# Folding the second sequence's odd rows a third time in a Fourier mixing kernel

## The chip, the cores and the metric

The kernel runs on one core of a Trainium2 chip. The metric is the device time of one execution in microseconds, the median of the runs.

## The reference

Eight sequences of 3008 rows and 256 columns go through a two-dimensional Fourier transform, of which the real part is kept, and then through a feed-forward layer with a squared ReLU:

```python
X = np.fft.fft(x, axis=1)            # x: 8 x 3008 x 256
X = np.fft.fft(X, axis=2).real
h = X.reshape(8 * 3008, 256) @ w_in  # 256 x 2048
r = np.maximum(h, 0.0)
out = (r * r) @ w_out                # 2048 x 256
```

## The kernel before

The transform along the columns is folded into the first weight matrix once, at the start (`G1`, `G2`, `gE`). What is left for each sequence b is the transform along the rows, for 1505 frequencies (the others mirror them). It gives three tiles: `Pt` (cosine part), `Qt` (sine part) and `Et` (one single column). They are allocated by `start`.

**Folding.** A row and its three mirror images arrive side by side in a tile `xt`. For each tile t, `fold(b, t)` makes five VectorE pieces (`s` at L420, `d` at L424, `sc` at L436, `dc` at L440 and `w` at L450, two instructions), and for some tiles a sixth, a `stream_shuffle` (L459). The result `folded[b, t]` has an even and an odd half, kp = 0 and 1. There are seven tiles in four classes: tile 0 (95 rows) and tile 1 (94) for classes 0 and 1, tiles 2 and 3 (`TWO`, 96 and 92) for class 2, and tiles 4 to 6 (`ODD0` on: 128, 128 and 120) for class 3, the odd rows. For b > 1 the odd rows come instead as four tiles 4 to 7 of 96 rows, two of them loaded in pieces of 32 and turned by the shuffle. Chains of VectorE and ScalarE pieces then fold them once more: `once` (pieces `begin`, `even`, `sine`, `odd`) and `twice` (`begin`, `even`, `sine`, `turned`, `copies`, `odd_v`, `odd_w`). `begin`, `sine` and `copies` are ScalarE work. Class 2 is folded by `once` in every sequence but the first. The chains are called `two`, `first` and `second` in `ahead`.

**The products.** `dft_ops(b)` makes a group of pieces for each part (which = 0 for `Pt`, 1 for `Qt`) and each kp: `even_n` and `odd_n` are matmuls into PSUM (tag "d", two buffers), and the joins (`join_4`, `join_2`, `join_1`, and `join_once`, `join_half`, `join_turned`) are VectorE work that reads them. `odd_n` multiplies class 3: for b = 1 by `product` (L567), three matmuls of 376 or 377 columns; for b > 1 by `twice_more` (L669), four of 94 or 95 columns. For that the table's columns are put in another order by `part_table` (ScalarE), after the last use in the old order. `dft_ops(None)` is the same transform for the single column of all later sequences at once; it reads `we`, which `scale_columns` (ScalarE) and `fold_columns` (VectorE, L398 and L400) make from 28 small loads (L391).

**The steps.** The feed-forward layer runs in 384 steps: 8 sequences x 6 blocks of 251 frequencies x 8 pairs of weight columns. In step i, `front` issues two halves h = 0 and 1, each with two matmuls into `ph` (L768, L769; two buffers) and three VectorE instructions (L771, L773, L774: the main work). ScalarE then does ReLU and square on `g` (L783, L784), GpSimd makes `s` (L791 to L794), and two steps later `back` issues seven matmuls (L821). After the last pair of a block, `gather` sums the products and two `store`s (transposes L887 and L888 on VectorE, then DMAs on SyncE's queue) follow in the steps with i % 8 equal to 3 and 4. Every matmul is in float32 and shows as two rows in the trace.

**What sets the order.** While sequence b runs, the pieces for b + 1 wait in a list `side`, written out by `ahead(b + 1)`. `between(h)` is called behind each half of `front` and takes pieces from the head of the list. Each has a nominal VectorE time. Zero-time pieces (matmuls, ScalarE work, allocations) are taken whenever they stand at the head on entry. The others are taken behind the second half of steps with a share, as long as the room of the slot and the pace allow; those in `from_psum` also elsewhere:

```python
SHARE = (1.2, 0.0, 0.0, 0.7, 0.7, 1.0, 1.0, 1.0)      # by i % 8
spent -= pace * share(i)                               # pace: sum of times / sum of shares
```

In the first sequence this begins with step 10, shares with step 12. All engines work through their instructions in the order in which they were issued. A tile load is issued on SyncE's queue by the `d` piece of an earlier tile (`load_later`, three ahead in the list `LATER`).

Of the kernel before, what the change touches and what calls it, by code (L numbers as in the profile page):

```python
# [82 lines left out]
def kernel(  # L83
# [13 lines left out]
    B, NROW, _, D = x.shape  # L97
# [11 lines left out]
    NT = len(TILES)  # L109
# [28 lines left out]
    ODD0 = NT - 3  # L138
    TWO = ODD0 - 2
# [12 lines left out]
    assert H == P and TILES[ODD0][0] == 3 and TILES[ODD0][3] >= ROWS2  # L152

    def load_x(b, t):
        if b > 1 and t >= ODD0:
            xt[b, t] = xp.tile([P, 4, D], F32, name="xt", tag="x")
            for p, first, count in ODD[t - ODD0]:
                nc.sync.dma_start(out=xt[b, t][p:p + count], in_=x[b, S // 8 + 1 + first:S // 8 + 1 + first + count])
            return
        c, r0, step, rows = TILES[t]  # L160
        if b and t == TWO + 1:
            xt[b, t] = xp.tile([P, 4, D], F32, name="xt", tag="x")
            for p in range(0, ROWS2, R):
                at = TILES[TWO][1] + step * (2 * HALF2 - p - R)
                nc.sync.dma_start(out=xt[b, t][p:p + R], in_=x[b, at:at + step * (R - 1) + 1:step])
            return

        while rows % 15 and rows % 16 and r0 + step * rows < NROW:
            rows += 1

        pool, tag = (gp, "g") if b == 0 and t < NT - NX else (xp, "x")
        xt[b, t] = pool.tile([P, 4, D], F32, name="xt", tag=tag)
        nc.sync.dma_start(out=xt[b, t][0:rows], in_=x[b, r0:r0 + step * (rows - 1) + 1:step])

    LATER = [(b, t) for b in range(1, B) for t in (TWO, TWO + 1, 0, *range(ODD0, NT if b == 1 else NL), 1)]

    def load_later(i):
        if i < len(LATER):
# [150 lines left out]
            tt(out=t4, in0=t2, in1=b21, op=ALU.subtract)  # L329


    folded, from_psum = {}, set()
    PQE = {}
    PART = (slice(0, H + 1), slice(H + 1, D))
    REVERSE = list(range(R - 1, -1, -1))
# [68 lines left out]
    def fold(b, t):  # L404


        odd, two = b > 1 and t >= ODD0, b > 0 and t == TWO + 1
        r = slice(0, ROWS2 if odd or two else TILES[t][3])
        st = {}

        def new(pool, nm, shape):
            st[nm] = pool.tile(shape, F32, name=nm, tag=nm)
            return st[nm]

        def f_s():
            nonlocal folds
            st["fs"] = sums[folds % 2]
            folds += 1
            v = xt[b, t]
            tt(out=st["fs"][r, :, 0:D], in0=v[r, 0::2], in1=v[r, 1::2], op=ALU.add)  # L420

        def f_d():
            v = xt[b, t]
            tt(out=new(fp, "fd", [P, 2, D])[r], in0=v[r, 0::3], in1=v[r, 1:3], op=ALU.subtract)  # L424
            if b > 0:
                load_later(LATER.index((b, t)) + NX)

        def halves():

            if b == 0 or "sc" not in st:  # L430
                st["sc"] = fp.tile([P, 2, D], F32, name="sc", tag="sc")
            return st["sc"]

        def f_sc():
            s = st["fs"]
            tt(out=halves()[r, :, PART[0]], in0=s[r, :, 0:H + 1], in1=s[r, :, D:H - 1:-1], op=ALU.add)  # L436

        def f_dc():
            d = st["fd"]
            tt(out=halves()[r, :, PART[1]], in0=d[r, :, 1:H], in1=d[r, :, D - 1:H:-1], op=ALU.subtract)  # L440

        def w_of(t):
            if (b, t) not in folded:
                folded[b, t] = wp.tile([P, 2, D], F32, name="w", tag="w")
            return folded[b, t]

        def f_w(part=slice(0, D)):
            v, w = st["sc"], w_of(t)
            for kp in range(2):
                tt(out=w[r, kp, part], in0=v[r, 0, part], in1=v[r, 1, part], op=ALU.subtract if kp else ALU.add)  # L450

        def f_e():
            nc.scalar.mul(lone[r, 2 * t:2 * t + 2, P - 1:], w_of(t)[r, :, H:H + 1], -1.0 if TILES[t][0] else 1.0)

        if b == 0:
            return [f_s, f_d, f_sc, f_dc, lambda: (f_w(PART[0]), f_e()), lambda: f_w(PART[1])]
        ops = [(0.7, f_s), (0.7, f_d), (0.5, f_sc), (0.4, f_dc), (0.9, f_w)]
        if odd and (t - ODD0) in (1, 2) or two:
            ops.append((0.7, lambda: nc.vector.stream_shuffle(w_of(t)[r], w_of(t)[r], REVERSE)))  # L459
        return ops  # L460
# [79 lines left out]
    def dft_ops(b):  # L540
# [7 lines left out]
        def group(kp, which):  # L548
# [138 lines left out]
            def odd_n():  # L687
                ps = psd.tile([P, 512], F32, name="pd", tag="d")[0:n]
                st["odd"] = ps[:, 0:n0]
                if b is None or b == 1:  # L690
                    return product(ps[:, 0:n0], 3)
                st["odd"] = twice_more(ps)

            def join_odd(what, nk):

                a, ps = st[what]
                nq = a.shape[-1]
                st[what] = o = hp.tile([P, NC[1][3]], F32, name="do", tag="do", bufs=1)[0:n, 0:nk]
                tt(out=o[:, 0::2], in0=a[:, 0:nq - 1], in1=ps[:, 0:nq - 1], op=ALU.add)
                if which == 1:  # L700
                    tt(out=o[:, 1::2], in0=ps[:, 1:nq], in1=a[:, 1:nq], op=ALU.subtract)
                else:
                    tt(out=o[:, 1::2], in0=a[:, 1:nq], in1=ps[:, 1:nq], op=ALU.subtract)
# [19 lines left out]
                return [((which, kp, nm), f) for nm, f in named]  # L723
            ops = [(0.0, even_n), (0.5, join_4), (0.7, join_2), (0.0, odd_n), (1.1, join_1)]
            from_psum.update((join_4, join_2, join_turned))
            join_once, join_half = (lambda: join_odd("odd", n0)), (lambda: join_odd("half", n1))
            from_psum.update((join_once, join_half))
            if b and b > 1:
                ops.insert(4, (0.7, join_once) if kp else (0.5, join_turned))
            if b and kp:  # L730
                ops.insert(2, (0.5, join_half))
# [22 lines left out]
    def load_e(b):  # L754
        nc.sync.dma_start(out=PQE[b][2], in_=e_dram[b:b + 1].to_broadcast([P, NKT]))
# [138 lines left out]

    def ahead(b):
        (_, start), *groups = dft_ops(b)
        tables = [(0.0, lambda tab=tab: part_table(tab, TWO if b == 1 else ODD0)) for tab in (cosT, sinT)]
        if b == 1:
            early = [(0.0, start), (0.0, take_turn), (0.5, make_turn)]
            middle = [(0.0, scale_columns), (1.0, fold_columns)] + dft_ops(None) + tables  # L900
        else:
            early, middle = tables if b == 2 else [], []
            groups = [(0.0, start)] + groups
        def woven(ops, chain):

            chain = list(chain)
            out = []
            for i, x in enumerate(ops):
                out += [x] + ([chain.pop(0)] if chain and i else [])
            return out + chain  # L910

        av, aw, bv, bw = range(ODD0, NL)

        def later(make):

            made = []

            def run(i):
                if not made:
                    made.extend(make())  # L920
                made[i]()

            return lambda times: [(x, lambda i=i: run(i)) for i, x in enumerate(times)]

        w = lambda t: folded[b, t]
        two = later(lambda: once(w(TWO), w(TWO + 1), BY_TWO))((0.0, 0.8, 0.0, 1.0))
        first = later(lambda: once(w(av), w(aw), BY_AC))((0.0, 0.8, 0.0, 1.0))
        second = later(lambda: once(w(bv), w(bw), BY_BD) + twice(w(av), w(aw), w(bv), w(bw)))(
            (0.0, 0.8, 0.0, 1.0, 0.0, 1.1, 0.0, 1.2, 0.0, 0.8, 0.8))
        if b == 1:  # L930
            return (early + fold(b, TWO) + fold(b, TWO + 1) + woven(fold(b, 0), two) + fold(b, ODD0) + middle
                    + fold(b, ODD0 + 1) + fold(b, ODD0 + 2) + fold(b, 1) + groups + [(0.0, lambda: load_e(b))])
        return (early + fold(b, TWO) + fold(b, TWO + 1) + woven(fold(b, 0), two) + fold(b, av) + fold(b, aw)
                + woven(fold(b, bv), first) + fold(b, bw) + woven(fold(b, 1), second)
                + groups + [(0.0, lambda: load_e(b))])

# [100 lines left out]
    def share(i):  # L1037
        return 0.0 if i < NJ + LAG + 2 else SHARE[i % NJ]

    def between(h):  # L1040


        nonlocal spent
        if i < NJ + LAG:
            return
        while side and not side[0][0]:
            side.pop(0)[1]()
        if h:
            spent -= pace * share(i)
        room = 1.9  # L1050
        while side and 0 < side[0][0] <= room and spent + side[0][0] / 2 <= 0:
            if not (h and share(i)) and side[0][1] not in from_psum:
                break
            t, f = side.pop(0)
            f()
            spent, room = spent + t, room - t

# [119 lines left out]
```

## Time and profile before

| | us |
|---|---|
| median of 3 runs | 1933.26 (1932.94 to 1933.3) |
| profiled execution | 1930.57 |
| its span | 1928.7 |
| TensorE busy | 1916.3 |
| VectorE busy | 1422.5 |
| GpSimd busy | 1105.5 |
| ScalarE busy | 950.3 |

The granted TensorE clock was 0.999. In the profile PE is the matmul part of TensorE and PEld its weight loads, which overlap matmuls; DVE is VectorE, ACT ScalarE, POOL GpSimd and SP SyncE. In a timeline a line gives the start in us, the duration in us, the engine, the source line and operation, output <- inputs with their shapes, the number of merged instructions, and in brackets the idle time before it with the engine and line that ended it. A matmul's duration includes its drain, so that neighbours overlap: the pace is read from start to start.

### The profile page before, as it was taken

The numbers are of one execution on the slowest core, as the hardware profiler recorded it, in microseconds if no ns is written. First come the engines' busy times: TensorE is split into PE (matmuls) and PEld (weight loads), VectorE is DVE, ScalarE is ACT, GpSimd is POOL, SyncE is SP. The second block draws the span as 40 slices with busy tenths as digits, with TensorE's granted clock in tenths as the row PEclk, the third lists the DMA queues.
The fourth block names the chain that finished last, engine by engine and source line by source line (L and its number), as shares of the span: only waits on it lengthen the run. The fifth ranks groups of instructions, "written<-read, shape, count | busy, mean of one in ns | idle before, by whom it ended". The sixth has DMA issues, their size and how long they took to land.

```text
span 1928.7 us, 28036 instructions
## 1 busy us (share of the span) xinstructions
PE 1916.3 (99%) x9258; PEld 1700.7 (88%) x9258; DVE 1422.5 (74%) x3595; ACT 950.3 (49%) x1179; POOL 1105.5 (57%) x1701
## 2 busy tenths in 40 slices
PE   9999999999999999999999999999999999999998
PEld 7888888888988888888988889888898888988887
DVE  8987767877677876787768777787777877655554
ACT  2855434555444554545444554445544555444443
POOL 0056555665566555666566565566656666566565
PEclk9999999999999999999999999999999999999999
DMA  7341111111111201121011110111111101100101
GB/s 225 115 43 32 33 23 45 36 28 31 28 36 28 47 12 29 35 47 28 12 35 36 39 28 12 44 39 36 21 18 47 36 12 22 28 12 12 22 12 22
DMA packets 145695, 69.53 MB, mean 36 GB/s; under 512 B 129228, under 2 KB 136342, under 8 KB 145549
## 3 DMA queue, kind: packets, MB, share of 16 engines
q1 hardware_dynamic: 145097, 66.83, 16.0%
q8 instruction: 73, 1.20, 0.3%
q14 instruction: 73, 0.60, 0.1%
q0 software_dynamic: 176, 0.65, 0.1%
q10 hardware_dynamic: 276, 0.26, 0.0%
HBM read 43.00 MB, written 24.69 MB: 35 GB/s over the span
## 4 chain that ended last, share of the span: by engine, by line
PE 95%; DVE 4%; issue 0%; DMA 0%; ACT 0%; DVEq 0%
PE ph L768 17%; PE ph L769 17%; PE mC L821 17%; PE mA L821 17%; PE mB L821 16%; PE mD L821 8%; PE pd L567 1%; PE pd L669 1%; PE pd L643 1%; DVE m L283 0%; DVE fd L281 0%; DVE w L450 0%; DVE he L771 0%; PE mA L808 0%; DVE fd L271 0%
## 5 line engine op out<-in xcount | busy, mean ns | idle before, releaser
L783 ACT ACTIVATE g<-g 128x1004 f32<-128x1004 f32 (+1 forms) x384 | 399.3, 1040 | 765.8 <-DVE g L774 445.0
L771 DVE SCALAR_TENSOR_TENSOR he<-Et,gE,ph 128x251 f32<-128x251 f32 (+1 forms) x768 | 363.0, 473 | 378.5 <-PE ph L769 373.4
L791 POOL TENSOR_TENSOR s<-g 128x251 f32<-128x251 f32 (+1 forms) x376 | 236.2, 628 | 686.5 <-ACT g L784 644.4
L768 PE MATMUL ph<-Pt,G 128*128 128x251 f32 (+1 forms) x1536 | 452.9, 376 | 0.0
L769 PE MATMUL ph<-Qt,G 127*128 127x251 f32 (+1 forms) x1536 | 452.0, 375 | 0.0
L784 ACT ACTIVATE g<-g 128x1004 f32<-128x1004 f32 (+1 forms) x384 | 399.3, 1040 | 12.2
L821 PE MATMUL mC<-s,wsum 128*128 128x251 f32 (+1 forms) x1504 | 381.7, 375 | 0.0
L821 PE MATMUL mA<-g,wout 128*128 128x251 f32 (+1 forms) x1504 | 380.0, 374 | 0.0
L773 DVE TENSOR_TENSOR g<-he,ph 128x251 f32<-128x251 f32 (+1 forms) x768 | 320.6, 417 | 53.3 <-POOL s L791 1.4
L769 PEld LDWEIGHTS ph<-Qt,G 127*128 127x128 f32 x1536 | 291.5, 190 | 35.8
L768 PEld LDWEIGHTS ph<-Pt,G 128*128 128x128 f32 x1536 | 285.7, 189 | 35.0 <-issue 0.6
L821 PEld LDWEIGHTS mC<-s,wsum 128*128 128x128 f32 x1504 | 285.6, 190 | 34.7
L821 PEld LDWEIGHTS mA<-g,wout 128*128 128x128 f32 x1504 | 282.9, 189 | 36.9 <-issue 1.3
L774 DVE TENSOR_TENSOR g<-he,ph 128x251 f32<-128x251 f32 (+1 forms) x768 | 314.3, 409 | 0.0
L792 POOL TENSOR_TENSOR s<-s,g 128x251 f32<-128x251 f32 (+1 forms) x376 | 270.4, 719 | 29.5
L793 POOL TENSOR_TENSOR s<-g 128x251 f32<-128x251 f32 (+1 forms) x376 | 271.4, 722 | 0.0
L794 POOL TENSOR_TENSOR s<-g,s 128x251 f32<-128x251 f32 (+1 forms) x376 | 238.7, 635 | 0.0
L821 PE MATMUL mB<-g,wsum 128*128 128x251 f32 (+1 forms) x752 | 220.5, 374 | 0.0
L821 PE MATMUL mD<-s,wout 128*128 128x251 f32 (+1 forms) x752 | 220.3, 374 | 0.0
L821 PE MATMUL mB<-s,wout 128*128 128x251 f32 (+1 forms) x752 | 219.9, 374 | 0.0
L821 PEld LDWEIGHTS mB<-g,wsum 128*128 128x128 f32 x752 | 142.6, 190 | 17.4
L821 PEld LDWEIGHTS mD<-s,wout 128*128 128x128 f32 x752 | 141.9, 189 | 17.7
(152 smaller groups left out, 1350.8 us busy)
## 6 DMA issues: line engine op xcount, KB each, us to landing
out_dram<-os SPq DMA_DIRECT2D x376, 56.0 KB
xt<-in_x_dram SPq DMA_DIRECT2D x37, 384.0 KB
xt<-in_x_dram SPq DMA_DIRECT2D x57, 128.0 KB
Et<-e_dram SPq DMA_DIRECT2D x7, 752.5 KB
out_dram<-os SPq DMA_DIRECT2D x288, 6.8 KB
raw<-in_moe_w_in_dram SPq DMA_DIRECT2D x16, 256.0 KB
raw<-in_moe_w_out_dram SPq DMA_DIRECT2D x16, 256.0 KB
xt<-in_x_dram SPq DMA_DIRECT2D x4, 512.0 KB
```

The source lines that it names most:

```text
L768: nc.tensor.matmul(hP, G1[:, fs], pt[:, ks], start=True, stop=True)
L769: nc.tensor.matmul(hQ, G2[0:P - 1, fs], qt[0:P - 1, ks], start=True, stop=True)
L771: nc.vector.scalar_tensor_tensor(out=t, in0=et[:, ks], scalar=gE[:, fc:fc + 1], in1=hP, op0=ALU.mult, op1=ALU.add)
L773: tt(out=g[:, h, 0, 0:n], in0=t, in1=hQ, op=ALU.add)
L774: tt(out=g[:, h, 1, 0:n][:, ::-1], in0=t, in1=hQ, op=ALU.subtract)
L783: act(v, v, AF.Relu)
L784: act(v, v, AF.Square)
L791: gt(out=s1, in0=g21, in1=g22, op=ALU.add)
L792: gt(out=s2, in0=s1, in1=g11, op=ALU.subtract)
L793: gt(out=s3, in0=g11, in1=g21, op=ALU.subtract)
L794: gt(out=s4, in0=g12, in1=s2, op=ALU.subtract)
L821: nc.tensor.matmul(acc[nm][:, i, 0:n], w, v[:, 0:n], start=j == 0 and i == 0, stop=j == NJ - 1, skip_group_check=True)
```

## The change

For b = 1 the odd rows take the path of the later sequences: four tiles of 96 rows, `once` and `twice` on them, `twice_more` in place of `product`, and the joins that go with it. The list for b = 1 becomes that of the others, with the column transform (`middle`) behind the first odd tile; `middle` now puts all four tables in the new order. `between` changes for all sequences: in its second loop zero-time pieces may follow at once in the same slot, save `even_n` and `odd_n` (the set `alone`), which still wait for the next call. In the first sequence a slot has room 2.4 in place of 1.9.

```diff
     def load_x(b, t):
-        if b > 1 and t >= ODD0:
+        if b and t >= ODD0:
...
-    LATER = [(b, t) for b in range(1, B) for t in (TWO, TWO + 1, 0, *range(ODD0, NT if b == 1 else NL), 1)]
+    LATER = [(b, t) for b in range(1, B) for t in (TWO, TWO + 1, 0, *range(ODD0, NL), 1)]
...
-    folded, from_psum = {}, set()
+    folded, from_psum, alone = {}, set(), set()
...
-        odd, two = b > 1 and t >= ODD0, b > 0 and t == TWO + 1
+        odd, two = b > 0 and t >= ODD0, b > 0 and t == TWO + 1
...
-                if b is None or b == 1:
+                if b is None:
                     return product(ps[:, 0:n0], 3)
                 st["odd"] = twice_more(ps)
...
             from_psum.update((join_4, join_2, join_turned))
+            alone.update((even_n, odd_n))
...
-            if b and b > 1:
+            if b:
                 ops.insert(4, (0.7, join_once) if kp else (0.5, join_turned))
...
-        tables = [(0.0, lambda tab=tab: part_table(tab, TWO if b == 1 else ODD0)) for tab in (cosT, sinT)]
+        tables = [(0.0, lambda tab=tab, t=t: part_table(tab, t)) for t in (TWO, ODD0) for tab in (cosT, sinT)]
         if b == 1:
             early = [(0.0, start), (0.0, take_turn), (0.5, make_turn)]
             middle = [(0.0, scale_columns), (1.0, fold_columns)] + dft_ops(None) + tables
         else:
-            early, middle = tables if b == 2 else [], []
+            early, middle = [], []
...
-        if b == 1:
-            return (early + fold(b, TWO) + fold(b, TWO + 1) + woven(fold(b, 0), two) + fold(b, ODD0) + middle
-                    + fold(b, ODD0 + 1) + fold(b, ODD0 + 2) + fold(b, 1) + groups + [(0.0, lambda: load_e(b))])
-        return (early + fold(b, TWO) + fold(b, TWO + 1) + woven(fold(b, 0), two) + fold(b, av) + fold(b, aw)
+        return (early + fold(b, TWO) + fold(b, TWO + 1) + woven(fold(b, 0), two) + fold(b, av) + middle + fold(b, aw)
                 + woven(fold(b, bv), first) + fold(b, bw) + woven(fold(b, 1), second)
                 + groups + [(0.0, lambda: load_e(b))])
...
-        room = 1.9
-        while side and 0 < side[0][0] <= room and spent + side[0][0] / 2 <= 0:
-            if not (h and share(i)) and side[0][1] not in from_psum:
+        room = 1.9 if i >= per else 2.4
+        while side and side[0][0] <= room and spent + side[0][0] / 2 <= 0:
+            t, f = side[0]
+            if f in alone or t and not (h and share(i)) and f not in from_psum:
                 break
-            t, f = side.pop(0)
+            side.pop(0)
             f()
             spent, room = spent + t, room - t
```

## The prediction

> **What bounds the kernel now.** I read the page first (its busy shares, then the chain that ended last), then a table of windows, one for each sequence, then the timeline of TensorE step by step, then VectorE around the places that the change fills. The page says that TensorE is the path:
>
> ```profile
> PE 1916.3 (99%) x9258; PEld 1700.7 (88%) x9258; DVE 1422.5 (74%) x3595; ACT 950.3 (49%) x1179; POOL 1105.5 (57%) x1701
> PE 95%; DVE 4%; issue 0%; DMA 0%; ACT 0%; DVEq 0%
> ```
>
> The windows say where it has no gap at all. Columns: window, then busy us and instructions of PE, PEld, DVE, ACT, POOL, the granted clock, the DMA share, GB/s:
>
> ```profile
> 60.00:300.00 240.00, 239.44 (x1134) 206.16 (x1133) 185.39 (x456) 124.21 (x168) 113.02 (x171) 1.00 0.24 49
> 300.00:540.00 240.00, 240.00 (x1163) 214.45 (x1162) 181.11 (x458) 121.28 (x151) 144.63 (x223) 1.00 0.14 31
> ```
>
> The reader is to see that the first sequence, from 60 us on, is as full as the second. So time is won only by taking TensorE work away, and lost only where TensorE is made to wait; VectorE has 55 us to spare in that window, on average.
>
> A busy TensorE hides its real pace, so I took the start of each step's first L768 matmul from the timeline. From step 12 (115.88 us) to the end, a step without transform matmuls takes 4.67 us, in every sequence. What a step takes above that is the price of the transform products in it. In the first sequence (which transforms the second one), steps 38 to 41, 44 and 46 take 0.89, 1.91, 2.80, 2.80, 0.88 and 1.89 us more: 11.17 us. In the second sequence, where the third one's odd rows are folded a third time, the sum is 1.79 + 0.90 + 0.90 + 0.89 + 0.89 + 0.88 + 0.88 = 7.13 us, and the four sequences after it have the same within 0.01. The difference lies in the odd products:
>
> ```profile
> 250.76 2.07 PE L567 MATMUL pd<-cosT,w 128*128 128x377 f32 x6
> 252.67 0.59 PE L768 MATMUL ph<-Pt,G 128*128 128x251 f32 x2
> ```
> ```profile
> 477.73 0.80 PE L669 MATMUL pd<-cosT,w 94*128 94x95 f32 x6
> 478.37 0.39 PE L669 MATMUL pd<-sinT,w 94*128 94x94 f32 x2
> 478.60 0.62 PE L821 MATMUL mA<-g,wout 128*128 128x251 f32 x2
> ```
>
> From start to start: three products of 377 columns (two rows each in the trace) take 1.91 us, four of 95 columns 0.87.
>
> **Part 1, TensorE.** `odd_n` for b = 1 goes from L567 to L669 in four groups (which 0 and 1, kp 0 and 1): 4 x (1.91 - 0.87) = 4.16 us. The step sums, which include the joints to the matmuls around, give 11.17 - 7.13 = 4.04 us; I take 4.04.
>
> A short product costs 0.109 us a row for 95 columns, against 0.318 for 377: so a thin product no longer pays by its columns.
>
> The Trainium skill ("TensorE: Matmul & The Clock Gate", "LDWEIGHTS (loading the stationary operand)") lets a weight load cost by its columns, 128/1.2 = 107 ns, however few rows, which speaks against thin folds; estimated by it the gain would be 4 x (1.91 - 8 x 0.107) = 4.2 us. By its streaming rule alone ("Back-to-back issue gap", N/2.4 + 2.5 ns), with two passes a row, it would be 4 x (1.91 - 0.67) = 5.0 us. The rows decide: 4.04.
>
> **Part 2, the pieces on VectorE.** Three folds of up to 128 rows become four of 96, with two shuffles, two `once`, one `twice` and four joins. I worked the rule of `between` through with both lists: the nominal sum for b = 1 rises from 41.2 to 55.7 us, the pace from 1.71 to 2.31 per unit of share, and with room 2.4 nearly every filled slot takes 1.6 to 2.3 nominal. In real time a slot can hold 2.3 us: 4.67 less two halves of main work at 1.17. What exceeds it makes VectorE late. TensorE bears some lateness: the second half's main work ends 3.46 us into its step (152.08 against 148.62), and its `ph` buffer is needed again at 4.67 + 0.85, so 2.1 us; `g` is done by ScalarE at 3.46 + 2.1 and is read by the back matmuls at 2 x 4.67 + 1.7, so over 5 us. So most slots cost nothing: the main work of the step covers them, and if that cover were gone the 15 us would be paid in part.
>
> One wait is tighter. The dealing rule moves the column transform (`scale_columns`, `fold_columns`, `dft_ops(None)`) from steps 25 to 30 to steps 21 to 24, and fills the slots ahead. Before, `fold_columns` stood alone in its slot:
>
> ```profile
> 189.84 0.26 DVE L398 TENSOR_TENSOR es<-xe 128x98 f32<-128x98 f32 x1
> 190.13 0.33 DVE L400 TENSOR_TENSOR we<-es 128x49 f32<-128x49 f32 x2
> 191.64 0.66 PE L567 MATMUL pd<-cosT,we 95*7 95x95 f32 x5
> ```
>
> `we` was ready 1.1 us before TensorE read it. After, I get: step 19 (`dc`, `w`, `two.odd`, then the store), step 20 (`s`, `d`, `sc`, store), step 21 (`dc`, `w`, `fold_columns`), and `even_n` behind the first front of step 22, where every `ph` matmul of the second front queues behind it on TensorE. Start from the same step 19 as now:
>
> ```profile
> 152.08 0.92 DVE L420 TENSOR_TENSOR fs<-xt 95x512 f32<-95x512 f32 x1
> 152.92 0.68 DVE L424 TENSOR_TENSOR fd<-xt 95x512 f32<-95x512 f32 x1
> 153.52 0.64 DVE L887 STREAM_TRANSPOSE os<-c 128x448 f32<-128x448 f32 x1
> 154.09 0.19 DVE L888 STREAM_TRANSPOSE os<-c 128x64 f32<-128x64 f32 x1
> 154.35 0.47 DVE L771 SCALAR_TENSOR_TENSOR he<-Et,gE,ph 128x251 f32<-128x251 f32 x1
> ```
>
> Mean paces from start to start over the trace: `s` 0.81, `d` 0.70, `sc` 0.45, `dc` 0.50, `w` 0.92, `once`'s odd 1.05, a store 0.78, the main work 2.34. Step 19: 152.08 + 0.50 + 0.92 + 1.05 + 0.78 = 155.33, one us later than the 154.35 above. Step 20: + 2.34 + 0.81 + 0.70 + 0.45 + 0.78 = 160.41. Step 21: + 2.34 + 0.50 + 0.92 + 0.29 + 0.2 = 164.66 for the half of `we` that is read first. TensorE comes to it at step 22 (162.65) + 0.85 = 163.50. It waits 1.2 us, and VectorE's main work for the second half comes that much later; by then VectorE has caught up, since step 22 lasts 7 us, and nothing is late next. With every op at its shortest pace there would be no wait, with every op at its longest 3.4 us; the ops are long and short by turns, so I take the means, 1.2, and 0.5 to 1.9 as likely.
>
> A second place: steps 35 to 39 hold `second`, where ScalarE's copies stand directly ahead of their VectorE readers. L509 and L510 take 0.46 us from start to last end, so VectorE waits some 0.6 in step 37 and 0.5 in step 38; its lateness grows 0.5, 1.2, 1.8, 2.2 over steps 35 to 38, and the last product of step 37's back, behind `sine`, relu and square on ScalarE and 2.65 us on GpSimd, comes within 0.2 of its due time. I take 0.2 lost, bounds 0 and 0.8. No gain is possible at either place: TensorE has no gap there now.
>
> **Part 3, what else moves.** All at nothing: the four tables (ScalarE, 1.7 us for two at 205.51, some 2.4 for the ODD0 pair that stood at 303.19) go to step 24, which lasts 8.1 us because two column products lie in it; uncovered they would hold back relu by 2 us, inside the 5. SyncE issues five more tile loads (eight for four tiles, in place of three), each after a `d`; its queue is behind until 138.90 us through the column loads (L391), and the first tile that comes this way is needed in step 20, at 157.7. The `e_dram` store and `load_e` go earlier. In later sequences, the zero-time pieces (`begin`, `sine`, `copies`) now run within a slot; worked through, no slot there exceeds 1.9 nominal, and VectorE is never more than 0.3 us late to a step there now.
>
> **Sum.** The profiled execution took 1930.57 us, of which 1928.7 span and 1.87 around it. -4.04 + 1.2 + 0.2 = -2.6: 1927.9 there. The median of the runs is 1933.26, 2.7 above the profiled one; the same difference gives 1930.6.
>
> **The rivals.** (a) Nobody waits: VectorE's ops come at their short paces, or the column transform lands a slot later than I dealt it. Then all 4.04 us show: 1929.2. For it: 55 us of free VectorE time. Against it: all the ops of three slots would have to be short at once.
> (b) Slower than before: ScalarE becomes the bound of the slots. Each zero-time piece that now runs within a slot (9 in the first sequence, 7 in each of six others) queues behind a relu and square pair of 2.1 us and VectorE waits for it with all behind it. It decides from where a slot plus its wait exceeds 2.3 + 2.1 us. If that cost TensorE 0.16 us for each of the 51, 8.0 us would go: 1933.3 - 4.0 + 8.0 = 1937.3. For it: the order on ScalarE is new everywhere. Against it: that pair ends about 1 us into the step, and the pieces run at 3.5.
> (c) The wait is larger: step 22 at 2.2, steps 37 to 39 at 0.8, and 1 us more in steps 28 to 32, which are as full: 1933.2, no difference.
>
> **How the numbers follow.** 0.2% is 3.87 us, about what a measurement of this kernel can tell from no change; (a) lies just beyond it, my sum within it. My sum with its bounds (1929.7 to 1931.9) has 0.55, (c) 0.15, (a) 0.20, (b) 0.10. Faster by over 0.2%: (a), 0.20. Within: 0.70. Slower: 0.10. The range reaches from (a) less 0.3 to (c) plus 1: 1928.9 to 1934.2.
>
> **What would show it.** Right: steps 38 to 47 carry 7.1 us above 4.67 each; a wait of PE for L400 near 163.6 of about 1.2 us; 24 fewer rows at L567 and 32 more at L669. Wrong: step 22 at 5.8 us (its product, no wait), or any gap of PE after 300 us.

## The result and the profile after

The changed kernel takes 1928.51 us (median of 13 runs, 1927.34 to 1929.80) against 1933.09 us for the kernel before (13 runs, 1931.24 to 1934.18): a ratio of 0.9977, 95% interval 0.9968 to 0.9985. It is faster by 4.6 us, 0.23% (by the interval, 2.9 to 6.2 us). The prediction was 1930.6 with a range from 1928.9 to 1934.2: the measured time lies 0.4 us below the range, and "faster by over 0.2%", which had 0.2, came true.

The profiled execution of the changed kernel took 1928.42 us, 1926.7 of them span. First the page: busy shares and instruction counts, then the shares of the chain that ended last.

```profile
PE 1912.0 (99%) x9266; PEld 1698.9 (88%) x9266; DVE 1444.1 (75%) x3633; ACT 956.0 (50%) x1201; POOL 1109.0 (58%) x1701
PE 95%; DVE 3%; DMA 1%; issue 0%; SPq 0%; ACT 0%; DVEq 0%
```

TensorE has eight rows more (32 at L669 in place of 24 at L567) and 4.3 us less busy time; VectorE has 22 us more and is still off the path. The windows (columns as before) miss 1.7 us of TensorE in the first sequence and nothing in the second. Cut finer, 1.5 us of that lie before 100 us (0.6 in the kernel before; step 10 begins 2.8 us later here), and 0.17 in step 22; from 170 us on there is no gap:

```profile
60.00:300.00 240.00, 238.30 (x1152) 206.94 (x1151) 202.40 (x502) 135.04 (x201) 115.56 (x172) 1.00 0.24 49
300.00:540.00 240.00, 240.00 (x1162) 214.47 (x1161) 182.47 (x458) 119.12 (x145) 144.94 (x224) 1.00 0.14 32
```

The timeline of TensorE, step 40 of the first sequence, has thin products where L567 stood with 377 columns:

```profile
258.49 0.62 PE L769 MATMUL ph<-Pt,G 128*128 128x250 f32 x2
258.95 0.59 PE L770 MATMUL ph<-Qt,G 127*128 127x250 f32 x2
259.37 0.80 PE L669 MATMUL pd<-cosT,w 94*128 94x95 f32 x6
260.01 0.39 PE L669 MATMUL pd<-sinT,w 94*128 94x94 f32 x2
260.24 1.04 PE L822 MATMUL mA<-g,wout 128*128 128x251 f32 x4
```

The four products take 0.87 us from start to start (259.37 to 260.24), as they did in the later sequences of the kernel before.

The two executions are compared by the starts of the steps, as in the prediction (line numbers behind the diff are one higher: `front` is L769 now). Excess over 4.674 us a step, in us:

| | before | after |
|---|---|---|
| transform products for the second sequence | 11.17 (steps 38 to 46) | 7.12 (steps 40, 41, 44 to 46) |
| column transform | 6.91 (steps 28, 29) | 7.16 (steps 22 to 24: 1.51, 2.20, 3.45) |
| steps 35 to 39 without products | 0 | 0 |
| start of step 10 to start of step 383 | 1803.91 | 1800.10 |
| start of step 383 to the end of the execution | 20.14 | 18.96 |

So -4.05 + 0.25 = -3.8 us in the steps, all of it before step 48 (from there to step 383 both take 1608.2 us), and -1.2 us behind them, of which the prediction knew nothing. (The last row counts the 1.8 us or so that the execution takes around its span; inside the span it is 18.26 and 17.20.) Together -5.0. The rest of the difference between two single executions is the start: step 10 began at 106.52 us in the kernel before and at 109.36 in the changed one. That start varies from execution to execution: over the traces below step 10 begins from 106.5 to 111.8 us with the old schedule (mean of six 109.0) and from 108.0 to 110.3 with the new one (mean of eight 108.8). No part of the gain is shown there.

Two questions were left. Why did TensorE wait 0.3 us for `we` and not 1.2? And are the 1.2 us at the end a part of the change?

### The profile page after: what moved, and what is told of

It reads as the page before. It is cut to its first block, busy times and chain, and to the rows that moved or that the text cites. A ratio compares the mean times of both kernels' runs of the same rounds, so it can differ in the third digit from the quotient of the medians.

```text
span 1926.7 us, 28110 instructions
## 1 busy us (share of the span) xinstructions
PE 1912.0 (99%) x9266; PEld 1698.9 (88%) x9266; DVE 1444.1 (75%) x3633; ACT 956.0 (50%) x1201; POOL 1109.0 (58%) x1701
## 4 chain that ended last, share of the span: by engine, by line
PE 95%; DVE 3%; DMA 1%; issue 0%; SPq 0%; ACT 0%; DVEq 0%
PE ph L769 17%; PE ph L770 17%; PE mC L822 16%; PE mA L822 16%; PE mB L822 16%; PE mD L822 8%; PE pd L567 1%; PE pd L669 1%; PE pd L643 1%; DMA cosT<-in_cos_s_dram 0%; DVE he L772 0%; DMA cosd<-in_cos_d_dram 0%; DVE m L283 0%; DVE fd L281 0%; DVE g L775 0%
## 5 line engine op out<-in xcount | busy, mean ns | idle before, releaser
L792 POOL TENSOR_TENSOR s<-g 128x251 f32<-128x251 f32 (+1 forms) x376 | 237.1, 631 | 692.4 <-ACT g L785 635.5
L769 PE MATMUL ph<-Pt,G 128*128 128x251 f32 (+1 forms) x1536 | 452.6, 375 | 0.0
L769 PEld LDWEIGHTS ph<-Pt,G 128*128 128x128 f32 x1536 | 285.3, 189 | 35.1 <-DVE g L775 1.1
L795 POOL TENSOR_TENSOR s<-g,s 128x251 f32<-128x251 f32 (+1 forms) x376 | 240.5, 640 | 0.0
```

The source lines that it names most:

```text
L769: nc.tensor.matmul(hP, G1[:, fs], pt[:, ks], start=True, stop=True)
L792: gt(out=s1, in0=g21, in1=g22, op=ALU.add)
L795: gt(out=s4, in0=g12, in1=s2, op=ALU.subtract)
```

## The experiments

**The new rule alone.** The kernel before, with only the diff's changes to `between`, to `alone` and to its two uses:

```diff
-        room = 1.9
+        room = 1.9 if i >= per else 2.4
...
+            if f in alone or t and not (h and share(i)) and f not in from_psum:
```

> The kernel before with the new rule of between alone (alone, room 2.4, zero-time pieces within a slot); the second sequence keeps its three odd tiles and the direct odd products. Theory 1 (TensorE's products are the whole gain): steps 38 to 46 still carry 11.17 us above 4.67 each, steps 22 to 29 6.9 us for the column transform, later sequences 7.13 each; time as before within 0.3 us. Theory 2 (the gain beyond 4.0 us comes from the rule, which lets ScalarE's pieces start earlier): 0.5 to 1 us faster than before. Rival (b) of the prediction (the rule makes VectorE wait for ScalarE in the slots): 1 us or more slower, and steps above 4.67 in the later sequences.

1932.12 us, ratio 0.9996 (0.9987 to 1.0005). Steps 10 to 383 take 1803.89 us, as before; the products take 11.17 in the same steps; the column transform moves to steps 25, 28 and 29 and takes 6.92. Rooms of 2.4 and zero-time pieces within a slot move work and cost nothing. The median is 0.9 us under that of the kernel before, as theory 2 had it, but not in the steps: the stretch behind the start of step 383 takes 18.91 us in place of 20.14, which the last experiments take up.

**The old rule in the later sequences.** The changed kernel, where zero-time pieces may follow within a slot in the first sequence only:

```diff
-            if f in alone or t and not (h and share(i)) and f not in from_psum:
+            if f in alone or i >= per and not t or t and not (h and share(i)) and f not in from_psum:
```

> The kernel after, but from the second sequence on zero-time pieces again wait for the next call, as before the change. Theory 1: nothing in the later sequences depends on it, 7.13 us above 4.67 in each and the same time as after, within 0.3 us. Theory 2: 0.5 to 1 us slower than after.

1927.34 us, ratio 0.9974 (0.9964 to 0.9985). Steps 10 to 383: 1800.11, as the changed kernel. With the run above this ends rival (b): the new order on ScalarE costs nothing that the steps show, in any sequence.

**The column transform one fold later.** It stands behind the second odd tile:

```diff
-                ... + woven(fold(b, 0), two) + fold(b, av) + middle + fold(b, aw)
+                ... + woven(fold(b, 0), two) + fold(b, av) + fold(b, aw) + middle
```

> The kernel after with the column transform one tile later in the list (behind tile 5 in place of tile 4): fold_columns is then dealt alone in step 24 and TensorE reads we in step 25, where VectorE is not late. Theory 1: the wait of 0.34 us for L400 is gone and the column transform costs 6.9 us in its steps in place of 7.16; the rest is the same; 0.3 us faster than after by the steps, too little for the runs to show. Rival (the 0.25 us more in steps 22 to 24 come from how the products are split over the steps, not from VectorE): still 7.1 to 7.2 us.

1927.57 us, ratio 0.9971 (0.9959 to 0.9982). `we` is ready at 177.9 us, nobody waits for L400, and the column transform takes 3.45 + 3.46 = 6.91 in steps 25 and 28. Steps 10 to 383: 1799.85, 0.25 less than the changed kernel. So the whole of the wait was worth 0.25 us. By its steps this version is the fastest of those that compute everything; the 0.25 is too small for the runs, where the one before has the lower median (1927.34).

**More VectorE work ahead of the two tight places.** `f_w` (two L450) is issued once more in the slot ahead of `we`, and twice more in step 38:

```diff
+        again = lambda ops: [(0.0, ops[4][1])] if b == 1 else []
+        f_av, f_1 = fold(b, av), fold(b, 1)
+        last = woven(f_1, second)
+        last = last[:-1] + again(f_1) * 2 + last[-1:]
-                ... + fold(b, av) + middle + fold(b, aw) + ...
+                ... + f_av + again(f_av) + middle + fold(b, aw) + ... + last
```

> The kernel after with the two instructions of L450 done once more in step 21, ahead of fold_columns, and twice more in step 38 (same values written again; nothing left out). If VectorE works at its short pace there (0.67 us for the pair), step 22 grows by 0.67 us, from 6.18 to 6.85; at the mean pace of the prediction (0.92) to 7.1; if TensorE did not wait for VectorE there it stays at 6.18. In step 38 the lateness at the start of step 39 grows from 1.55 us by 1.35 to 1.85; by the prediction's count of ph buffers what exceeds 2.4 us is lost, 0.5 to 1.0 us around steps 39 and 40; if the tolerance is larger, nothing.

1933.33 us (one run). Step 22 rises from 1.51 to 2.62; steps 39 and 40 carry 2.54 and 3.55 in place of 0 and 1.79, so 4.3 us. Both costs are above what was expected (0.67 to 0.9 and 0.5 to 1.0): both places were sensitive, but the size depends on what stands beside the added work. The timeline of VectorE at both places:

```profile
164.88 1.42 DVE L450 TENSOR_TENSOR w<-sc 96x256 f32<-96x256 f32 x4
...
166.51 0.78 DVE L400 TENSOR_TENSOR we<-es 128x49 f32<-128x49 f32 x2
...
255.23 3.33 DVE L450 TENSOR_TENSOR w<-sc 94x256 f32<-94x256 f32 x4
```

The same four instructions took 1.42 us in step 21 and 3.33 in step 38, and the pair L400 0.78 in place of the 0.33 it takes in the changed kernel. GpSimd and TensorE in the second place:

```profile
255.85 0.81 POOL L795 TENSOR_TENSOR s<-g,s 128x251 f32<-128x251 f32 x1
256.62 0.81 POOL L792 TENSOR_TENSOR s<-g 128x251 f32<-128x251 f32 x1
257.51 0.77 POOL L793 TENSOR_TENSOR s<-s,g 128x251 f32<-128x251 f32 x1
...
259.85 0.69 PE L769 MATMUL ph<-Pt,G 128*128 128x250 f32 x2 [2.37 <-DVE g L775]
```

GpSimd ran one instruction after the other beside the slow four; beside the quick four it was idle (an instruction ended at 164.57, the next began at 166.47). The last line measures the tolerance: VectorE came 4.80 us late to step 39 (its main work began 5.85 us behind the step's first matmul, in an undisturbed step 1.05) and TensorE waited 2.37, so the `ph` buffer of the first half forgives 2.4 us (the prediction worked out 2.1 for the second).

**GpSimd silent.** The changed kernel without GpSimd's L792 to L795 in the first sequence; `back` reads `g` there:

```diff
+        if i < per:
+            return g.rearrange("p a b n -> p (a b) n")
```

> The kernel after, but in steps 8 to 47 GpSimd's combination (L792 to L795) is left out and the back matmuls read g in place of s; the rest of the first sequence is issued as in after. Theory (VectorE instructions with two SBUF inputs take their short pace, 0.60, 0.33 and 0.34 us, when GpSimd is idle and up to twice that when they meet one of its instructions): dc at the head of steps 19 and 21 falls from 0.69 and 0.81 us to 0.33, we comes some 0.8 us earlier, the wait of 0.34 us in step 22 is gone (6.9 us above 4.67 in steps 22 to 24 in place of 7.16), VectorE starts step 39 less than 1.2 us late in place of 1.55. Rival (the first instruction behind L775 is slow because L774 and L775 read PSUM ahead of it): dc stays at 0.69 to 0.81, the wait stays within 0.1 us.

1928.29 us (one run). Steps 10 to 383: 1799.99. Slot 21 of VectorE, to be read beside that of the changed kernel further down:

```profile
163.45 0.41 DVE L440 TENSOR_TENSOR sc<-fd 96x254 f32<-96x254 f32 x1
163.89 0.76 DVE L450 TENSOR_TENSOR w<-sc 96x256 f32<-96x256 f32 x2
164.57 0.25 DVE L398 TENSOR_TENSOR es<-xe 128x98 f32<-128x98 f32 x1
164.86 0.33 DVE L400 TENSOR_TENSOR we<-es 128x49 f32<-128x49 f32 x2
```

`dc` at the head of the slot takes 0.41 us in place of 0.77; lateness at the starts of steps 20 and 21 falls from 0.57 and 0.41 to 0.26 and 0.10, and at step 39 from 1.55 to 0.26; the wait for L400 is gone and the column transform takes 6.93. The rival, which put the long `dc` down to VectorE's own reads of PSUM ahead of it, would have kept it. The pieces of slot 20 keep their paces (0.60, 0.60, 0.34 and 0.69 for the store, against 0.60, 0.61, 0.33 and 0.69): there GpSimd did not hinder them in the changed kernel either.

**Both together.** The added work of the run before the last, and GpSimd silent (the two diffs above in one).

> The kernel with the repeated work in steps 21 and 38, and again without GpSimd's combination in steps 8 to 47 (left out, g read in place of s). Theory: the four L450 in step 38, 3.3 us beside GpSimd, take 1.35 us; VectorE starts step 39 some 2.3 us late, within the 2.4 that the ph buffers allow, and the 4.3 us lost in steps 39 and 40 fall below 0.3; step 22 loses at most 0.2 us. Rival: the four keep 2.5 us or more and TensorE loses 1.5 us or more in step 39.

1928.60 us (one run). The four L450 of step 38 take 1.42 us (3.33 beside GpSimd), VectorE is 1.60 us late to step 39, and steps 39 and 40 carry no wait: 11.13 us together, against 15.43 with GpSimd at work and 11.14 in the changed kernel. Step 22 still loses 0.17. So 4.3 us of TensorE's time hung on whether GpSimd worked beside these four VectorE instructions and the pieces ahead of them (without the added work the lateness at step 39 is 1.55 us with GpSimd and 0.26 without).

**Both kernels again.** For the end of the run, the kernel before and the changed kernel without any edit:

> The kernel before, unchanged, measured like the others: a ratio of 1.000 with an interval that says what such a comparison can resolve, and a second profile of the start. Theory (the start varies from execution to execution, the steps do not): step 10 begins anywhere between 105 and 113 us, and from there to the start of the last step it takes 1803.9 us within 0.1, as in the first profile. Rival (the steps vary as well): more than 0.3 us of difference between the two profiles.

1933.64 us, ratio 1.0001 (0.9992 to 1.0010); steps 10 to 383 in 1803.92, end 20.20 us.

> The kernel after, unchanged. By the steps it is 3.81 us faster than before (1800.10 against 1803.91 us from step 10 to step 383), so 0.9980; the first comparison gave 4.6 us. If the 0.8 us more are the scatter of the start, the median falls between 1928 and 1930.5 and the ratio between 0.9970 and 0.9988, and the profile again shows 1800.1 us between these steps with step 10 anywhere between 105 and 113 us. If after starts earlier by itself, step 10 begins near 108.5 again and the ratio stays at or below 0.9977.

1927.81 us against 1933.18, ratio 0.9972 (0.9962 to 0.9982); steps in 1800.11, end 19.08 us. Steps and ends repeat; what varies is the start.

**ScalarE's instructions shifted.** The end differs in one place: the last store's two DMA issues on ScalarE's queue. In the kernel before, and in the changed one:

```profile
1923.59 2.44 ACTq L879 DMA_DIRECT2D out_dram<-os  x2
```
```profile
1922.62 1.09 ACTq L880 DMA_DIRECT2D out_dram<-os  x2
```

In the kernel before, a packet of the queue q14, of the kind `instruction`, falls into that stretch. DMA queues between 1923.5 and 1926.1 us (packets, MB, share of the 16 engines):

```profile
q1 hardware_dynamic: 283, 0.26, 33.4%
q10 hardware_dynamic: 66, 0.07, 7.9%
q14 instruction: 1, 0.01, 1.6%
```

Three kernels shift ScalarE's stream by instructions that write the same small values again at 109 us (nine or eighteen more of L344, 0.19 us each), and a control adds six on VectorE (L350):

```diff
-                nc.scalar.mul(turn[r, a, i:i + 1], ...)
+                for _ in range(2):                        # range(3) for eighteen
+                    nc.scalar.mul(turn[r, a, i:i + 1], ...)
```
```diff
-            tt(out=to, in0=u, in1=v, op=op)
+            for _ in range(3):
+                tt(out=to, in0=u, in1=v, op=op)
```

> The kernel before, with nine more ScalarE instructions that write the same values again (each instruction of take_turn, L344, is issued twice; 0.19 us each, near 109 us). It tells whether the last 1.2 us of the gain belong to the change. By the steps the changed kernel wins 3.8 us; the rest of what was measured lies behind the start of step 383, where the kernel before takes 20.14 and 20.20 us to the end and the changed one 18.9 to 19.1. There ScalarE's two last DMA issues take 2.44 and 2.54 us against 1.09, and a packet of the instruction queue falls between them. Theory F (instruction fetch): ScalarE's stream of instructions is fetched in pieces, and a piece ends between the two issues in the kernel before; nine more instructions ahead move that point. Steps 10 to 383 as before, 1803.9 us (bound 0.3), the two issues 1.1 us, the end 19.0 us: 1.1 us faster than before. Rival W (the work): the longer end goes with the schedule of the kernel before, whatever ScalarE's stream is: 2.4 to 2.5 us for the issues and 20.1 to 20.2 for the end, time as before. Both: no other step changes.

1931.31 us against 1933.16, ratio 0.9991 (0.9982 to 1.0001). By the runs alone this is no sure difference, and the steps are those before (1803.92), but the end falls from 20.14 to 18.77 us. ScalarE's queue, then the DMA queues from 1925.0 to 1927.5 us:

```profile
1925.07 1.09 ACTq L880 DMA_DIRECT2D out_dram<-os  x2
```
```profile
q1 hardware_dynamic: 283, 0.26, 34.9%
q10 hardware_dynamic: 276, 0.26, 33.5%
```

No packet of q14 there, and the issues take 1.09 us.

> As the run with nine more ScalarE instructions, with eighteen (each of L344 is issued three times). Theory F: the point between two pieces moves further; the two issues take 1.1 us and the end 19.0 us, unless the point falls on them again. Rival W: 2.4 to 2.5 us and 20.1 to 20.2 us. Steps 10 to 383: 1803.9 us by both, up to 0.5 more if 3.4 us of ScalarE work at step 10 holds a relu back.

1930.00 us (one run): steps 1803.91, issues 1.09, end 18.82 us.

> The changed kernel with eighteen more ScalarE instructions (each of L344 is issued three times). Theory F: a shift of ScalarE's stream alone can make the end longer or leave it; two sizes of shift in the kernel before and one here, so a long end (issues of 2 us or more, end of 19.8 to 20.2) here would show that the schedule has no part in it. Rival W: the end stays at 18.9 to 19.1 us. Steps 10 to 383: 1800.1 us by both.

1929.39 us (one run): steps 1800.09, issues 1.10, end 19.00 us. This shift met no packet, so by itself it tells neither theory from the other.

> Control: the kernel before, with six more instructions on VectorE in place of ScalarE (each of make_turn, L350, is issued three times, 0.15 us each, near 119 us). If the fetch in question is that of ScalarE's stream, the end stays at 20.1 to 20.2 us and the two issues at 2.4 to 2.5 us. If any change in the program moves it (fetches of all engines share the queue), it may go to 19.0. Steps 10 to 383: 1803.9 us.

1933.83 us (one run): steps 1803.91, end 20.32 us. ScalarE's queue, and q14 between 1926.6 and 1929.1 us:

```profile
1926.67 2.39 ACTq L880 DMA_DIRECT2D out_dram<-os  x2
```
```profile
q14 instruction: 1, 0.01, 1.7%
```

All fourteen traces, with the stretch from 0.3 us ahead of the two issues to 1.8 us behind their start:

| kernels | q14 packet there | two issues, us | end, us |
|---|---|---|---|
| before, before again, six more on VectorE | yes | 2.44, 2.54, 2.39 | 20.14, 20.20, 20.32 |
| before with the rule alone, with 9, with 18 | no | 1.08, 1.09, 1.09 | 18.91, 18.77, 18.82 |
| changed, again, old rule later, `we` later, more work, 18 | no | 1.08 to 1.10 | 18.96 to 19.08 |
| GpSimd silent, and with more work | yes | 1.96, 2.21 | 19.77, 20.04 |

The long end comes with both schedules and leaves the old one when nine ScalarE instructions are added. So the last 1.2 us are no work that the change saved: they come and go with the packet. In the five traces that have it there, the packet begins between 0.21 us ahead of the start of the first of the two issues and 0.38 behind it, so beside the first and not between the two; that first issue takes 1.30 to 1.88 us in place of 0.38, the second 0.62 in place of 0.67. The other queue of this kind, q8, has no packet that begins within 4 us of them in any of the fourteen. Whether the packet itself holds the issue up, and whether it carries ScalarE's instructions, no run tests apart. Which counts of which instructions put the packet there is open too: the rule alone removed it with the same 1179 busy instructions on ScalarE, and the kernels with GpSimd silent brought it back with the changed kernel's 1201.

## Why the prediction was wrong

**Part 1 was right.** -4.04 was worked out from two step sums, and -4.05 came.

**The wait for `we` was the mis-sized term**: 1.2 us, measured 0.34 (by the pace of the matmul ahead TensorE was due at 166.34 and started at 166.68), of which 0.25 shows in the steps. The place, the step and the instructions were as worked out. VectorE in the changed kernel:

```profile
154.92 0.65 DVE L440 TENSOR_TENSOR sc<-fd 95x254 f32<-95x254 f32 x1
155.61 0.76 DVE L450 TENSOR_TENSOR w<-sc 95x256 f32<-95x256 f32 x2
156.29 0.87 DVE L495 SCALAR_TENSOR_TENSOR w<-w,turn,f 94x256 f32<-94x256 f32 x2
...
160.05 0.68 DVE L420 TENSOR_TENSOR fs<-xt 96x512 f32<-96x512 f32 x1
160.65 0.68 DVE L424 TENSOR_TENSOR fd<-xt 96x512 f32<-96x512 f32 x1
161.26 0.42 DVE L436 TENSOR_TENSOR sc<-fs 96x258 f32<-96x258 f32 x1
...
164.64 0.77 DVE L440 TENSOR_TENSOR sc<-fd 96x254 f32<-96x254 f32 x1
165.45 0.76 DVE L450 TENSOR_TENSOR w<-sc 96x256 f32<-96x256 f32 x2
166.12 0.25 DVE L398 TENSOR_TENSOR es<-xe 128x98 f32<-128x98 f32 x1
166.41 0.33 DVE L400 TENSOR_TENSOR we<-es 128x49 f32<-128x49 f32 x2
```

and TensorE, which waits for the first half of `we` (the 0.17 in the line counts from the end of the drain of the matmul ahead):

```profile
166.68 1.14 PE L567 MATMUL pd<-cosT,we 95*7 95x95 f32 x8 [0.17 <-DVE we L400]
```

The changed kernel's step 19 starts 2.85 us later than that of the kernel before (151.47 against 148.62), so the prediction's walk starts at 152.08 + 2.85 = 154.93; `dc` began at 154.92. From there, in us (from each start to the next):

| stretch | predicted | measured |
|---|---|---|
| slot 19: `dc`, `w`, odd and store | 0.50 + 0.92 + 1.83 = 3.25 | 0.69 + 0.68 + 1.48 = 2.85 |
| step 20: main work, `s`, `d`, `sc`, store | 2.34 + 0.81 + 0.70 + 0.45 + 0.78 = 5.08 | 2.28 + 0.60 + 0.61 + 0.33 + 0.69 = 4.51 |
| step 21: main work, `dc`, `w`, `es`, half of `we` | 2.34 + 0.50 + 0.92 + 0.29 + 0.2 = 4.25 | 2.36 + 0.81 + 0.67 + 0.29 + 0.2 = 4.33 |
| sum | 12.58 | 11.69 |

0.89 us too much, and 1.2 - 0.89 is the 0.3 that came. The failed step is the choice of means for the pieces. For those with two inputs in SBUF a mean over the whole trace mixes two kinds of slots: short where GpSimd is idle (`s` 0.60, `sc` 0.33, `w` 0.67), long beside it. Those kinds don't come by turns at random, as I took them to. (Of the 0.89, 0.18 are the two stores, at 0.69 in place of 0.78. They take 0.69 with GpSimd silent too; why the mean is higher was not looked into.) Around slots 19 to 21, GpSimd's four instructions have ended before the slot begins or within 0.5 us of its start, and the next step's begin only when VectorE's main work and ScalarE are done:

```profile
159.35 0.63 POOL L795 TENSOR_TENSOR s<-g,s 128x251 f32<-128x251 f32 x1
162.44 0.63 POOL L792 TENSOR_TENSOR s<-g 128x251 f32<-128x251 f32 x1 [2.46 <-ACT g L785]
```

All of slot 20 (160.05 to 162.28) lies in the gap between these two, 159.98 to 162.44; in slots 19 and 21 only the `dc` at the head meets an L795 (in slot 19 the store's transposes meet an L792 as well and keep their 0.64 and 0.20 us). This is no rule for late slots: VectorE is 0.59 us late to step 37, and there GpSimd runs on for 1.8 us of the slot, so that L495 takes 1.33 us in place of 0.87:

```profile
246.75 1.33 DVE L495 SCALAR_TENSOR_TENSOR w<-w,turn,f 94x256 f32<-94x256 f32 x2
246.86 0.95 POOL L794 TENSOR_TENSOR s<-g 128x251 f32<-128x251 f32 x1
247.76 0.81 POOL L795 TENSOR_TENSOR s<-g,s 128x251 f32<-128x251 f32 x1
```

The lateness grows on there, to 1.02 us at step 38 and 1.55 at step 39. The argument against rival (a), "all the ops of three slots would have to be short at once", fell on this: they are short together, because one thing makes them so. (a), at 1929.2, was the nearest case and had 0.20.

GpSimd's part is shown by the runs with GpSimd silent: `dc` 0.41 in place of 0.77, four L450 1.42 in place of 3.33. The Trainium skill ("SBUF — State Buffer", "🔬 SBUF: two separate sides") has a rule for it, not used in the prediction: a VectorE instruction with two inputs in SBUF and a GpSimd instruction that reads SBUF shut each other out for their whole length. The rows agree in that the two alternate: an L450 needs 0.34 us alone and some 0.8 beside GpSimd, about one for each GpSimd instruction (0.77 to 0.89 us there, 0.63 to 0.72 alone). They don't show the whole length: 0.34 and some 0.7 in turn would be 1.0 us for each pair, and 0.8 was measured, so the two records overlap a little.

**Steps 35 to 39 were to lose 0.2 and lost 0.** VectorE came 1.55 us late to step 39, where the prediction had 2.2 after step 38; the measured tolerance of 2.4 covers both.

**Part 3 was right** for what it named: tables, tile loads, ScalarE's pieces and the later sequences cost nothing (steps 48 to 383 within 0.1 us).

**Nothing in the sum looked at the end of the program**, the 20 us behind the start of the last step, and the range's low end stood 0.3 us below rival (a) for all that the steps don't hold. The end alone was worth 1.2. By the steps the prediction was 1.2 us off (-2.6 against -3.8); the end more than accounts for the rest of the 2.1 us by which the median was off, and "faster by over 0.2%" came true with its help: -3.8 us alone lies just inside the 3.87 us of 0.2%.

## What to carry to other kernels

Don't cost a chain of VectorE instructions by means over a trace when GpSimd works beside it: take the short row where GpSimd is idle and the long one where it runs, and lay the chain over GpSimd's own timeline. A late chain can be cheap, where the engine that would hinder it has finished by then (slots 20 and 21), or dear, where that engine is late as well (slots 37 and 38). Where a few us decide, compare the stretches ahead of the first and behind the last repeated step by themselves in several executions before calling a difference a gain of the change.

## What the runs showed of the hardware

A packet of the queue q14 (`instruction`) beside the first of ScalarE's last two DMA issues comes with 1.96 to 2.54 us for the two, against 1.08 to 1.10 without it (fourteen traces, no exception), and most of that reaches the end of the run: 19.77 to 20.32 us from the start of step 383, against 18.77 to 19.08. It appears and goes with edits that change no work there, so two versions of a program can differ by 1.2 us (0.06% here) for this alone.

Beside GpSimd's elementwise instructions on 251 columns a VectorE addition or subtraction of two SBUF operands of 94x256 in float32 took 0.8 us in place of 0.34, and GpSimd's own grew from 0.63 and 0.72 to between 0.77 and 0.90. 0.7 us of added VectorE work in step 21 cost TensorE 1.1 us at step 22, and 1.4 us of it (at the short pace) cost 4.3 us at steps 39 and 40; with GpSimd silent the same work cost 0.17 us and nothing.
